# Fixed buffers in place of rotating pools, and a reordered instruction table, in an attention and MLP kernel on one core

## The chip, the core and the metric

The kernel runs on one core of a Trainium2 chip. The metric is the device time of one execution in microseconds (us). The engines named below are PE (TensorE, with PEld for its weight loads), DVE (VectorE), ACT (ScalarE), POOL (GpSimd) and SP (SyncE, which here only issues DMAs).

## The reference

```python
def _attn_ref(q, k, v):
    q_s = np.exp(q - np.max(q, axis=-1, keepdims=True))
    q_s = q_s / (np.sum(q_s, axis=-1, keepdims=True) + 1e-09)
    k_s = np.exp(k - np.max(k, axis=2, keepdims=True))
    k_s = k_s / (np.sum(k_s, axis=2, keepdims=True) + 1e-09)
    kv = np.einsum('bhsd,bhse->bhde', k_s, v)
    return np.einsum('bhsd,bhde->bhse', q_s, kv)      # 8 x 8 heads, 576 rows, 64 columns
def _moe_ref(x, w_in, w_out):                         # x: 4608 x 512, w_in: 512 x 2048
    h = x @ w_in
    sp = np.where(h > 20.0, h, np.log1p(np.exp(np.minimum(h, 20.0))))
    return (h * np.tanh(sp)) @ w_out                  # Mish, then 2048 x 512
```

The output of the attention, with its heads side by side, is x. All inputs are float32.

## The kernel before, in words

**The work.** The attention goes item by item (two heads each, numbers 0 to 31 in the names q16, k16, pkv6 and so on). A query item is loaded (q_load, L346, on SP), its row maxima are reduced on DVE (L392, `qm`), exchanged and subtracted (ACT L379, DVE L383, POOL L224), raised to the exponential (ACT L470, with an ACT table load ahead of it), summed, divided, transposed (DVE L510 and its neighbours) and multiplied on PE (L538, tiles `px` and `pt`). The key side is similar: kt_load (L335, tile `kt_two`, on SP), the exponential on ACT (L458, L473), the product with v on PE (L573, tile `pkv`).

The MLP works on 9 chunks of 512 rows. Each float32 operand is split in a high and a low float32r part, and each product takes three matmuls (high by high, high by low, low by high). Three chunks go through the first product directly (h_part, L629). The other six, in three pairs k = 1 to 3, go through a scheme that computes a 2 by 2 block product with seven block products: first_product (L823) makes the partial products `px`, `py` and `pz` in PSUM, ACT copies them into `g` (L859), DVE adds others (L863), ACT applies Mish (L867). second_product (L839, tiles `qx`, `qy`, `qz`) does the same for w_out, with k = 0 to 3. Its operand `gs` is made from `g`: a mix on DVE where needed (g_mix, L224, `g<-g,g`), a high part on ACT (CAST, L889), a low part on DVE (L224, `gs<-g,gs`). One call of first_product or second_product for one block is six matmuls of 512 columns, which the text calls a product.

**The weights.** The sums of weight blocks that the seven products need (`w_in`, `m_in`, `w_out`, `m_out`: POOL L739, ACT L743, DVE L224) are stored once to a DRAM array `ws` (L704, on SP) and come back by w_fetch (L807, on POOL's own DMA queue) into a ring of six buffers: a fetch waits until PE has read what its buffer held.

**The order.** Nothing here is scheduled automatically. ORDER is a table of 2522 tokens (for example `A1.3.5`: first_product of block 3, product 5, pair 1; `BB0.2.1`: second_product; `LQ16`: the load of q16; `F88`: the fetch of ws88; `GH1.1.1`: the high part of `gs1_1_1`; `DS0.2.1`: a store of output; `LK30`: the load of k30). The program goes through it once, so the table sets the order of the instructions on each engine; across engines they wait on semaphores. BANKS is a second table, of letters, that gives each PSUM tile one of eight banks.

**The pools touched.** Pool `sp` rotates 4 buffers of the tag "wc", first for the unpacked weights (`wc_*`), then for output tiles (`ob*`). Pool `wp` rotates 2 buffers for `m0_*` and `m1_*`. Pool `rp` rotates 4 for `gh*` and 4 for `gl*`. open_sc (token `PS`) closes the pools `rw`, `sp`, `wp` and `rq` and opens the rings s1, s2, s3 and s0, which hold the `gs` tiles of the pairs 1 to 3, in their memory. The first write into that memory, the ACT CAST of `gs1_1_1` (token `GH1.1.1`), waits for the last readers of the closed pools, among them the stores of the `ob0_*` tiles.

Of the kernel before, what the change touches and what calls it, by code (L numbers as in the profile page):

```python
# [33 lines left out]
RB16 RA18 RO14 WK0 RB15 RM20 R31 RB18 RH17 RC16 RM21 QZ5 H29 RA19 RO17 RC15 H30 RH16 RB19 R26 RH15 H31 RC19 QM4 O5  # L34
RC18 Y7 RA23 RO16 RA21 RH18 RB21 RA24 RO18 RC21 O6 RM24 RB23 RB24 RO15 QM5 RC23 H32 RC24 H33 G7 RH24 H34 GL7 RH19 RO24
MK7 H35 MK6 T4 RL26 Y8 O7 RD19 LQ6 TC4 G8 R28 RA20 R27 GL8 RH23 LK8 RB20 RM25 RO23 ST2 RC20 RA22 V6 H40 RH21 RS22 RB22
T5 RO21 H41 RC22 LQ7 TC5 H42 RA25 RH20 RB25 H43 RH22 RO20 RC25 H36 MQ6 R29 RH25 H37 L6 Y10 RD22 H38 RA26 SQ6 G10 WK9
H39 RB26 H44 Y9 RO25 RC26 H45 GL10 H46 RL28 WW8v EQ6 H47 GA9 Q6 XT4 O8 WM8.0p ZT4 RA27 GL9 RM27 ZT5 WM8.1p RA28 RB27
ST5 RM30 RC27 WK8 RH26 O9 MQ7 RB28 SQ7 RC28 WK6 QZ6 EQ7 QM6 H48 WH8.0 Q7 RH28 H49 RO26 WH8.1 H50 RH27 H56 WL8.1 QZ7
RO28 H52 WP8.1 H57 Y11 WL8.0 GA11 H51 QM7 MK8 WP8.0 H58 Y12 WK10 RO27 H53 GA12 GL11 KB8 GL12 H54 WW9v RM29 H59 RA29  # L40
WK12 H55 Y14 RB29 B6 Y13 O10 KS6 GA13 WM9.0p WK1 GL13 WH9.0 WM9.1p RC29 RW30 O11 ST4 GA14 RL31 RB30 RH29 RC30 RW31 KM8
GL14 WL9.0 XP4 RB31 UE8.0 WP9.0 RD29 T6 RH30 RC31 O12 WH9.1 Z5 WL9.1 Z4 WP9.1 TC6 ZL4 EK6 ZL5 WW10v T7 KP6 LQ8 TC7
# [5 lines left out]
LK12 WM12.1p GM20 WH12.0 PK8 WH12.1 WL12.0 WW13v WP12.0 PX8 WL12.1 HM19 EQ10 Z9 LQ11 Q10 Z8 WP12.1 ZL9 MK12 V12 ES0.3
HM31 GM19 ZT9 WM13.0p QW10 QV10 WH13.0 MQ11 QM10 HM16 KB12 ZL8 MS11 T10 WM13.1p WH13.1 MT11 WL13.0 HM26 S10 SQ11
WP13.0 WL13.1 ST9 EQ11 GH0.1.1 LQ12 Q11 WP13.1 HM30 KM12 WW14v UE12.1 WK7 QW11 ZT8 QV11 UE12.0 HM24 QM11 ST8 U12.0 T11  # L50
WM14.0p GM26 MQ12 GM22 U12.1 GM16 HM17 WM14.1p GM24 LK14 ES0.2 WW15v PX10 GM17 WH14.0 PK10 MS12 WL14.0 WP14.0 Z11 HM21
Z10 ZL11 WH14.1 MT12 ZL10 SQ12 ZT10 S12 WL14.1 EQ12 HM40 LQ13 Q12 WP14.1 QW12 WM15.0p GH0.1.0 HM32 GK0.1.1 MK14 GM30
# [1007 lines left out]
```

## Time and profile before

| | before |
|---|---|
| median of 3 runs | 781.46 us (780.98 to 783.69) |
| profiled execution, its own time | 782.3 us |
| its span | 780.5 us |
| granted TensorE clock | 1.000 throughout (2.4 GHz) |
| PE busy | 770.3 us, 99% of the span |
| DVE, ACT, POOL busy | 563.7 us (72%), 511.0 us (65%), 297.3 us (38%) |
| moved by DMA | 192.75 MB, 247 GB/s on average |

Shares are of the span, and an engine counts as busy while one of its instructions runs. PE fills the span almost whole, so the place to look is the few gaps between its instructions.

### The profile page before, as it was taken

To read this page: it belongs to the slowest core of one execution; us is meant where nothing else is said; L and a number is where in the kernel's file an instruction comes from. 1 tells how busy PE (TensorE), PEld (TensorE's weight loads), DVE (VectorE), ACT (ScalarE), POOL (GpSimd) and SP (SyncE) were. 2 spreads that over 40 slices of the span, in tenths; PEclk is the share of its full clock that TensorE was granted. 3 is DMA by queue.
4 is the path that set the end of the run, shared out by engine and by line. 5 is a ranking of instruction groups with operands and counts; after the bars stand their busy time and mean duration, and the time that the engine had idled before them with its cause. 6 is when DMAs were issued, how large, how long until landed. Compare 5 with 4: busy or idle time off the path is not lost.

```text
span 780.5 us, 12662 instructions
## 1 busy us (share of the span) xinstructions
PE 770.3 (99%) x4592; PEld 623.5 (80%) x4592; DVE 563.7 (72%) x877; ACT 511.0 (65%) x952; POOL 297.3 (38%) x378
## 2 busy tenths in 40 slices
PE   8999999999999999999999999999999999999997
...
PEclk9999999999999999999999999999999999999999
...
GB/s 342 399 347 234 299 270 267 229 169 249 267 295 300 293 304 207 311 325 254 218 212 234 239 299 174 236 188 232 191 235 202 252 227 190 163 237 170 240 202 175
DMA packets 80717, 192.75 MB, mean 247 GB/s; under 512 B 16016, under 2 KB 28560, under 8 KB 80656
## 3 DMA queue, kind: packets, MB, share of 16 engines
...
q8 instruction: 36, 0.59, 0.3%
...
## 4 chain that ended last, share of the span: by engine, by line
PE 68%; DVE 9%; ACT 7%; DMA 7%; issue 4%; POOL 3%; SPq 1%; DVEq 0%; POOLq 0%; ACTq 0%
PE px L823 15%; PE qx L839 14%; PE qy L839 8%; PE qz L839 8%; PE py L823 7%; PE ph L629 6%; PE pz L823 4%; DMA ws<-ws 2%; PE po L670 2%; DMA q<-in_qs_dram 2%; DVE gs L224 2%; PE px L538 1%; DMA ws<-m_in 1%; PE pt L573 1%; POOL m_in L739 1%
## 5 line engine op out<-in xcount | busy, mean ns | idle before, releaser
L807 POOL DMA_DIRECT2D ws<-ws x200 | 108.5, 544 | 373.5 <-PE px L823 78.0
L889 ACT CAST gs<-g 128x1024 fp32r<-128x1024 f32 x112 | 116.4, 1052 | 75.4 <-PE qx L839 26.3
L224 DVE TENSOR_TENSOR gs<-g,gs 128x1024 fp32r<-128x1024 f32 x112 | 137.3, 1242 | 37.0 <-ACT gs L889 36.8
L839 PE MATMUL qx<-gs,ws 128*128 128x512 f32 x576 | 136.2, 390 | 0.2 <-DVE gs L224 0.2
L823 PE MATMUL px<-xh,ws 128*128 128x512 f32 x384 | 128.9, 392 | 0.8 <-ACT g L859 0.5
L839 PEld LDWEIGHTS qx<-gs,ws 128*128 128x128 f32 x576 | 107.9, 188 | 23.9 <-issue 0.8
L839 PE MATMUL qz<-gs,ws 128*128 128x512 f32 x384 | 92.2, 391 | 0.7 <-DVE gs L224 0.7
L839 PE MATMUL qy<-gs,ws 128*128 128x512 f32 x384 | 90.9, 390 | 0.3 <-DMA ws<-ws 0.2
L629 PE MATMUL ph<-xs,wi 128*128 128x512 f32 x384 | 90.2, 391 | 0.0
L823 PEld LDWEIGHTS px<-xh,ws 128*128 128x128 f32 x384 | 72.1, 188 | 18.5 <-ACT g L859 1.9
L839 PEld LDWEIGHTS qz<-gs,ws 128*128 128x128 f32 x384 | 71.7, 188 | 16.9 <-DVE gs L224 1.1
L839 PEld LDWEIGHTS qy<-gs,ws 128*128 128x128 f32 x384 | 71.9, 188 | 16.1 <-DMA ws<-ws 0.6
L629 PEld LDWEIGHTS ph<-xs,wi 128*128 128x128 f32 x384 | 71.6, 188 | 16.0 <-issue 1.0
L859 ACT COPY g<-px 128x512 f32<-128x512 f32 x72 | 41.2, 586 | 64.2 <-PE px L823 64.1
L224 DVE TENSOR_TENSOR g<-g,g 128x1024 f32<-128x1024 f32 x64 | 78.3, 1235 | 3.7 <-ACT g L867 2.9
L823 PE MATMUL px<-xl,ws 128*128 128x512 f32 x192 | 74.9, 390 | 0.0
L823 PE MATMUL py<-xh,ws 128*128 128x512 f32 x192 | 65.9, 389 | 0.0
L863 DVE TENSOR_TENSOR g<-py,g 128x512 f32<-128x512 f32 x48 | 32.2, 682 | 41.0 <-PE py L823 20.8
L224 POOL TENSOR_TENSOR q<-q,qm 128x576 f32<-128x576 f32 (+1 forms) x31 | 42.3, 1364 | 29.2 <-DVE qm L383 15.6
L867 ACT ACTIVATE g<-g 128x512 f32<-128x512 f32 x72 | 43.5, 629 | 6.4 <-DVE g L863 6.0
L629 PE MATMUL ph<-xs_odd,wi 128*128 128x512 f32 x192 | 45.1, 391 | 0.0
L629 PEld LDWEIGHTS ph<-xs_odd,wi 128*128 128x128 f32 x192 | 35.8, 188 | 8.3 <-issue 0.8
(169 smaller groups left out, 1267.7 us busy)
## 6 DMA issues: line engine op xcount, KB each, us to landing
ws<-ws POOLq DMA_DIRECT2D x197, 512.0 KB, 4.6
...
ws<-m_out SPq DMA_DIRECT2D x32, 256.0 KB, 2.7
ws<-m_in SPq DMA_DIRECT2D x32, 256.0 KB, 3.8
raw_out<-in_w_dram SPq DMA_DIRECT2D x14, 512.0 KB, 7.7
...
ws<-wi SPq DMA_DIRECT2D x24, 256.0 KB, 5.3
```

The source lines that it names most:

```text
L224: eng.tensor_tensor(out, a, b, ALU.subtract)
L538: nc.tensor.matmul((px, pt)[x][h][o], kvt[a, j], at[e + j]["qT"][x][a], start=True, stop=True)
L573: nc.tensor.matmul(pkv[i][j * D:(j + 1) * D], k, v_two[a, j, c], start=c == 0, stop=c == NR - 1)
L629: nc.tensor.matmul(gs[n], wi[f][:, a, t], x[:, z], start=t == 0 and i == 0, stop=t == HP - 1 and i == 2)
L670: nc.tensor.matmul(po[t], g[a][:, t * P:(t + 1) * P], wo[f][:, z], start=f == 0 and i == 0, stop=f == NF - 1 and i == 2)
L807: nc.gpsimd.dma_start(dst, src)
L823: nc.tensor.matmul(dst, w[:, a, j], xc[k, p][z][:, j].rearrange("p b s -> p (b s)"), start=p in (1, 2, 7) and j == 0 and i == 0, stop=j == ...
L839: nc.tensor.matmul(psb[key, k][m], w[:, a, m], g[z][:, f % 2], start=first and i == 0, stop=f == NH - 1 and i == 2, skip_group_check=p in ...
L859: nc.scalar.copy(g_quad(k, n)[q], psb[1, k, n])
L863: nc.vector.tensor_tensor(g, psb[2 if q == 0 else 7, k, n], g, ALU.add)
L867: nc.scalar.activation(g, psb[1, k, n] if q == 1 else g, AF.Mish)
L889: nc.scalar.copy(t[0], gq[k, h][G_PART[p]])
```

## The change

The rotating pools are replaced by buffers with fixed numbers: a table SLOTS gives each unpacked weight, output tile and `gh`/`gl` tile the one of four buffers that it takes, and the two `wp` buffers are named m0 and m1 instead of turned. The pools hold as many buffers as before. ORDER keeps its first 300 tokens; behind them the same 2222 tokens stand in another order, on average 14 places from where they stood. BANKS has the same letters up to the 69th and others behind. The instructions are the same in number and kind on every engine: PE has 3886 matmuls in both, 3120 of them of 512 columns. 95 of 1282 tiles lie at another address. Lines of the changed file have numbers higher by 5.

```diff
 ORDER = """
...
-WM10.0p OP13.0 V8 S6 WK13 OP13.2 WH10.0 RD30 XT6 U8.0 WM10.1p XP6 ZT6 ZT7 MQ8 OP14.0 ST7 Z6 WL10.0 WH10.1 ST6 OP13.3
...
+OP13.0 LQ8 TC7 WW10v V8 OP14.0 U8.0 XT6 WM10.0p XP6 ZT6 ZT7 ST7 H60 Z7 ST6 WM10.1p Z6 H61 WH10.0 ZL6 H62 UE8.1 ZL7
...
+SLOTS = {"in": "0321330310321010", "out": "0212021323323021", "ob": "3021", "g": "0321032102310231"}
+
+
+def slot(kind, n):
+    return SLOTS[kind][n]
...
-    plain = [tc.tile_pool(name="rw", bufs=1), tc.tile_pool(name="sp", bufs=4)]
+    plain = [tc.tile_pool(name="rw", bufs=1), tc.tile_pool(name="sp", bufs=1)]
...
-        a = sp.tile([P, SM], U32, tag="wc", name=f"wc_{kind}{f}")
+        a = sp.tile([P, SM], U32, tag=f"wc{slot(kind, f)}", name=f"wc_{kind}{f}")
...
-        plain.append(tc.tile_pool(name="wp", bufs=2))
+        plain.append(tc.tile_pool(name="wp", bufs=1))
...
-        plain.append(tc.tile_pool(name="rp", bufs=LAG + 1))
+        plain.append(tc.tile_pool(name="rp", bufs=1))
...
-        hi = pools["rp"].tile([P, SM], F32R, tag="rh", name=f"gh{n}")
+        hi = pools["rp"].tile([P, SM], F32R, tag=f"rh{slot('g', n)}", name=f"gh{n}")
...
-        ob = obs[c, t] = sp.tile([P, DM], F32, tag="wc", name=f"ob{c}_{t}")
+        ob = obs[c, t] = sp.tile([P, DM], F32, tag=f"wc{slot('ob', t)}", name=f"ob{c}_{t}")
...
-        m = mixed[j, s] = pools["wp"].tile([P, 2, 2, 2 * P], F32, tag="st", name=f"m{s}_{kind}{f}")
+        m = mixed[j, s] = pools["wp"].tile([P, 2, 2, 2 * P], F32, tag=f"st{s}", name=f"m{s}_{kind}{f}")
```

What the two tables do to the engines, at three places. In these rows a name ends in the program's own buffer number, which differs between the two kernels, and the changed kernel's line numbers are higher by 5.

**DVE, at the low part of `gs0_2_1_1`**, in the first quarter of the second products of k = 0. `qm16` is the row maximum of q16, `g...` a mix, `m...` a weight sum, `rs14` and `kvt` the end of an item's key side, `qT15` and `odd` transposes. Before:

```order
L492 RECIPROCAL qs15_2776<-qs15_2776 128x18
L509 STREAM_TRANSPOSE qT15_2832<-qe15_2771 128x512
L510 STREAM_TRANSPOSE odd_88<-qe15_2771 128x64
L392 TENSOR_REDUCE qm16_2845<-q16_2778 128x18
L224 TENSOR_TENSOR g0_2_1_2363<-g0_2_3_2560,g0_2_1_2363 128x1024
L224 TENSOR_TENSOR gs0_2_1_1_2848<-g0_1_2_2056,gs0_2_1_0_2847 128x1024
L224 TENSOR_TENSOR m0_in2_2811<-m0_in2_2811 128x2x256
L224 TENSOR_TENSOR gs0_2_2_1_2861<-g0_2_2_1803,gs0_2_2_0_2860 128x1024
```

After:

```order
L229 TENSOR_TENSOR g0_2_1_2371<-g0_2_3_2481,g0_2_1_2371 128x1024
L397 TENSOR_REDUCE qm16_2823<-q16_2724 128x18
L468 STREAM_TRANSPOSE k16_2832<-kt_two_114 128x576
...
L592 RECIPROCAL rs14_2842<-rs14_2842 128x2
...
L514 STREAM_TRANSPOSE qT15_2860<-qe15_2718 128x512
L515 STREAM_TRANSPOSE odd_88<-qe15_2718 128x64
L388 TENSOR_TENSOR qm16_2823<-qm16_2823,sm16_2834 128x18
L229 TENSOR_TENSOR gs0_2_2_1_2858<-g0_2_2_2091,gs0_2_2_0_2857 128x1024
L229 TENSOR_TENSOR gs0_2_1_1_2820<-g0_1_2_2225,gs0_2_1_0_2819 128x1024
```

Before, the low part of `gs0_2_1_1` stands two rows behind the reduce of q16; in the change it stands twelve rows behind. The load of q16 (token `LQ16`) has moved too: between it and the reduce PE has five products before, and a group of 12 more matmuls of h_part on top in the change.

**POOL, at the fetch of ws88**, near the end of the second products of k = 1. `qe27` is a division and `q28` a subtraction of the attention, `ws` rows are fetches. Before:

```order
L496 TENSOR_TENSOR qe27_5145<-qe27_5145,qs27_5163 128x576
L807 DMA ws86_5207<-ws_109 128x1024
L807 DMA ws87_5233<-ws_109 128x1024
L807 DMA ws88_5259<-ws_109 128x1024
L224 TENSOR_TENSOR q28_5154<-q28_5154,qm28_5222 128x576
L807 DMA ws89_5369<-ws_109 128x1024
L807 DMA ws90_5388<-ws_109 128x1024
```

After:

```order
L812 DMA ws86_5208<-ws_109 128x1024
L501 TENSOR_TENSOR qe27_5149<-qe27_5149,qs27_5168 128x576
L812 DMA ws87_5228<-ws_109 128x1024
L812 DMA ws89_5331<-ws_109 128x1024
L229 TENSOR_TENSOR q28_5163<-q28_5163,qm28_5250 128x576
L812 DMA ws88_5351<-ws_109 128x1024
L812 DMA ws93_5384<-ws_109 128x1024
L812 DMA ws91_5394<-ws_109 128x1024
```

The fetches of ws88 and ws89 have changed places, and the subtraction for q28 stands ahead of ws88. On SP, the load of k30 (576 KB) is issued right ahead of the fetch of ws88 in the table before, and two attention steps and four products ahead of it in the change.

**ACT, at the high part of `gs1_1_1`**, in the first products of k = 1. `g1_*` rows are copies out of PSUM and Mish, `sm`, `kw` and `sz` small exchanges of the attention. Before:

```order
L867 ACT_TABLE_LOAD
L867 ACTIVATE g1_1_3_3875<-g1_1_3_3875 128x512
L601 COPY xt20_4310<-pt20_0_4157 128x64
L379 COPY sz22_4312<-qs22_4300 32x18 x4
L867 ACTIVATE g1_2_1_4074<-px1_4_4017 128x512
L859 COPY g1_3_2_4288<-px1_6_4257 128x512
L767 COPY raw2_4265<-px21_4204 128x512
L867 ACTIVATE g1_1_0_3872<-g1_1_0_3872 128x512
L889 CAST gs1_1_1_4346<-g1_1_0_3872 128x1024
L867 ACTIVATE g1_2_0_4073<-g1_2_0_4073 128x512
L867 ACTIVATE g1_2_1_4074<-px1_5_4081 128x512
```

After:

```order
L864 COPY g1_2_0_4021<-px1_5_4034 128x512
L384 COPY kw24_4077<-km24_4042 32x4 x4
L872 ACTIVATE g1_0_3_3739<-g1_0_3_3739 128x512
L864 COPY g1_1_3_3843<-px1_3_3935 128x512
L872 ACTIVATE g1_0_3_3739<-g1_0_3_3739 128x512
L872 ACTIVATE g1_1_0_3840<-g1_1_0_3840 128x512
L894 CAST gs1_1_1_4108<-g1_1_0_3840 128x1024
L872 ACTIVATE g1_1_1_3841<-px1_2_3815 128x512
L864 COPY g1_2_2_4023<-px1_4_4006 128x512
L475 ACT_TABLE_LOAD
L475 ACTIVATE qe21_4124<-q21_3859 128x576
L864 COPY g1_2_3_4024<-px1_4_4006 128x512
```

The CAST of `gs1_1_1` stood behind the work on `px1_6` and now stands right behind that on `px1_4` and `px1_5`, some 20 products earlier in the run of first products; the Mish of `g1_1_1` and two copies out of `px1_4` come right behind it. What it waits for stands on SP, in the change as follows (`m0_in5` and `m1_in5` are weight sums on their way to `ws`, two DMAs each, and `ob0_2_1` is an output tile of the pool `sp`):

```order
L340 DMA kt_two_114<-in_kp_dram 128x1152
L709 DMA ws_109<-m0_in5_3912 128x512 x2
L709 DMA ws_109<-m1_in5_3981 128x512 x2
L927 DMA out_1_dram<-ob0_2_1_3254 128x512
L351 DMA q22_4134<-in_qs_dram 128x576
L361 DMA v3_113<-in_v2_dram 128x1188
```

The store of `ob0_2_1` is issued behind the two stores of `m1_in5`, which wait for that tile's low part on DVE; in the table its token stands right ahead of `PS`, and four products (`A1.4.7`, `A1.3.5`, `A1.2.3`, `A1.4.6`) stand between it and `GH1.1.1`. One more product (`A1.3.3`) stands between `GH1.1.1` and `A1.4.5`, which writes the bank of `px1_4` again and so needs the copy `g1_2_2` out of it, two rows behind the CAST.

## Rows read from the trace of the kernel before

**Rows 1.** The page: the span, the busy time of PE, and PE and its granted clock over the span in 40 slices (tenths).

```profile
span 780.5 us, 12662 instructions
...
PE 770.3 (99%) x4592; PEld 623.5 (80%) x4592; DVE 563.7 (72%) x877; ACT 511.0 (65%) x952; POOL 297.3 (38%) x378
...
PE   8999999999999999999999999999999999999997
...
PEclk9999999999999999999999999999999999999999
```

**Rows 2.** A piece of the chain that ended last, all of it PE: start, us, engine, tile, line, count.

```profile
267.62 9.52 PE qx L839 x42
```

**Rows 3.** What PE waited for, the three largest but those of the first 12 us: total us, times, longest us.

```profile
PE pz L823 <- DMA ws<-ws: 1.2, 1, 1.2
...
PE qz L839 <- DVE gs L224: 0.7, 1, 0.7
PE px L823 <- ACT g L859: 0.5, 2, 0.3
```

**Rows 4.** The timeline of PE at all its waits behind the first 12 us, with a row more around two of them: start us, us, engine, line, operation, tiles, shape, count, and in brackets the idle time ahead of it and what released it.

```profile
106.54 1.28 PE L573 MATMUL pkv<-v,k 64*64 64x66 f32 x72 [0.34 <-ACT k L473]
...
230.52 0.98 PE L839 MATMUL qz<-gs,ws 128*128 128x512 f32 x3 [0.69 <-DVE gs L224]
...
257.99 0.74 PE L839 MATMUL qx<-gs,ws 128*128 128x512 f32 x2 [0.23 <-DVE gs L224]
...
336.96 0.47 PE L823 MATMUL px<-xh,ws 128*128 128x512 f32 x1 [0.28 <-DMA ws<-ws]
...
346.34 0.39 PE L823 MATMUL py<-xh,ws 128*128 128x512 f32 x1
347.01 0.50 PE L823 MATMUL px<-xh,ws 128*128 128x512 f32 x1 [0.28 <-ACT g L859]
347.35 0.39 PE L823 MATMUL px<-xl,ws 128*128 128x512 f32 x1
...
374.49 0.50 PE L823 MATMUL px<-xh,ws 128*128 128x512 f32 x1 [0.27 <-ACT g L859]
...
465.21 0.47 PE L823 MATMUL pz<-xh,ws 128*128 128x512 f32 x1 [1.19 <-DMA ws<-ws]
...
763.14 1.52 PE L839 MATMUL qz<-gs,ws 128*128 128x512 f32 x6
764.75 0.96 PE L839 MATMUL qy<-gs,ws 128*128 128x512 f32 x3
...
772.74 0.73 PE L839 MATMUL qy<-gs,ws 128*128 128x512 f32 x2 [0.22 <-DMA ws<-ws]
```

**Rows 5.** The timelines of SP (the first row, the issue of the load of q16) and of DVE: its wait for that load and what stood behind; then a reduce of q17.

```profile
220.23 1.00 SPq L346 DMA_DIRECT2D q<-in_qs_dram  x1
...
227.44 0.75 DVE L392 TENSOR_REDUCE qm<-q 128x18 f32<-128x576 f32 x1 [2.12 <-DMA q<-in_qs_dram]
228.12 1.22 DVE L224 TENSOR_TENSOR g<-g,g 128x1024 f32<-128x1024 f32 x1
229.25 1.22 DVE L224 TENSOR_TENSOR gs<-g,gs 128x1024 fp32r<-128x1024 f32 x1
...
256.06 0.74 DVE L392 TENSOR_REDUCE qm<-q 128x18 f32<-128x576 f32 x1
```

**Rows 6.** Two fetches: an issue on SP (k30), then the piece of the chain that is the fetch of ws88 behind it (start, us); then the issue of ws43 on POOL.

```profile
456.28 0.33 SPq L335 DMA_DIRECT2D kt_two<-in_kp_dram  x1
...
456.58 8.50 DMA ws<-ws
...
328.94 0.53 POOL L807 DMA_DIRECT2D ws<-ws  x1 [1.12 <-PE px L823]
```

**Rows 7.** DMA issues (kind, count, KB each, median us from issue to landing): of the whole span, and in the last row of the stretch from 333 to 346 us alone.

```profile
ws<-ws POOLq DMA_DIRECT2D x197, 512.0 KB, 4.6
...
out_dram<-ob SPq DMA_DIRECT2D x19, 256.0 KB, 4.7
...
out_dram<-ob SPq DMA_DIRECT2D x3, 256.0 KB, 7.5
```

**Rows 8.** The timeline of ACT: ahead of PE's two waits for a copy out of PSUM (347.01 and 374.49), and ahead of the one for `pkv` (106.54).

```profile
345.85 0.63 ACT L867 ACTIVATE g<-g 128x512 f32<-128x512 f32 x1
346.39 0.57 ACT L859 COPY g<-px 128x512 f32<-128x512 f32 x1
...
373.27 0.69 ACT L470 ACTIVATE qe<-q 128x576 f32<-128x576 f32 x1 [1.21 <-POOL q L224]
373.87 0.57 ACT L859 COPY g<-px 128x512 f32<-128x512 f32 x1
...
105.29 1.20 ACT L473 ACTIVATE k<-k 128x1152 f32<-128x1152 f32 x1
```

**Rows 9.** The timeline of DVE ahead of PE's start at 764.75.

```profile
764.01 0.68 DVE L918 TENSOR_TENSOR g<-qy,g 128x512 f32<-128x512 f32 x1
```

**Rows 10.** The page's groups of instructions: line, engine, operation, tiles, count, busy us, mean ns of one, idle time ahead and what ended most of it.

```profile
L889 ACT CAST gs<-g 128x1024 fp32r<-128x1024 f32 x112 | 116.4, 1052 | 75.4 <-PE qx L839 26.3
...
L859 ACT COPY g<-px 128x512 f32<-128x512 f32 x72 | 41.2, 586 | 64.2 <-PE px L823 64.1
```

More of the change, by code (lines that the diff above doesn't have):

```diff
@@ L33 @@
 RO13 RA17 RA14 RS17 RO12 QZ4 O3 RB14 RB17 Y5 RL23 GA5 RC17 Y6 RC14 RL19 GA6 H28 GL5 R25 O4 RS18 RA16 GL6 RA15 RH14
[L34 to L42, printed above, removed]
@@ L48 @@
[L48 to L52, printed above, removed]
@@ new lines @@
+A1.7.2 F55 C1.6.2 QV22 F58 J1.5.2 QM22 A1.7.6 J1.7.0 N1.5.2 MQ23 A1.7.7 J1.6.0 C1.7.2 MS23 A1.6.5 N1.5.3 MT23 T22
+N1.0.2 GX1.2.0v N1.7.0 BB1.0.1 F59 C1.6.3 SQ23 BB1.1.1 EQ23 A1.7.5 LQ24 Q23 GH1.2.0 F62 F60 J1.6.3 QW23 BB1.2.1
+GK1.2.0 C1.7.3 QV23 A1.6.3 GX1.1.0v A1.6.4 N1.6.1 J1.7.3 QM23 MK26 A1.7.3 F61 MQ24 F63 BB1.3.1 T23 N1.7.1 N1.3.2
+GX1.1.1v BB1.4.1 GH1.2.1 F64 N1.6.0 GK1.2.1 PK22 MS24 GH1.1.3 MT24 J1.6.2 PX22 SQ24 V26 N1.4.3 BB1.5.1 GK1.1.3
+GX1.2.1v A1.7.4 EQ24 ZT22 ST22 BB1.6.1 J1.7.2 LQ25 Q24 N1.7.2 BB1.7.1 GX1.0.1v QW24 F66 F65 N1.7.3 GX1.3.0v BB1.0.2
@@ new lines @@
+GH1.2.2 QV24 XR22 BB1.1.2 S24 N1.6.2 QM24 BB1.2.2 GH1.7.0 GK1.2.2 F67 GH1.2.3 GK1.7.0 BB1.3.2 F68 N1.6.3 GK1.2.3
+BB1.4.2 GH1.7.1 MQ25 BB1.0.7 GK1.7.1 F69 MS25 MT25 BB1.5.2 T24 SQ25 GX1.0.2v EQ25 BB1.6.2 GH1.7.2 LQ26 GX1.3.1v
+BB1.7.2 F70 GK1.7.2 BB1.1.7 GH1.7.3 F71 Q25 GX1.1.2v ZT23 KB26 BB1.2.7 ST23 DP1.0.0 KM26 GH1.6.0 DJ1.0.0 BB1.3.7
+DS1.0.0 UE26.1 GK1.6.0 BB1.4.7 DP1.0.1 GK1.7.3 QW25 BB1.0.6 F73 UE26.0 QV25 MQ26 GH1.6.1 QM25 BB1.5.7 DJ1.0.1 MS26
+DS1.0.1 GX1.2.2v F72 BB1.6.7 GK1.6.1 GH1.6.2 BB1.1.6 F74 XR23 T25 GK1.6.2 BB1.2.6 MT26 U26.0 SQ26 BB1.3.6 U26.1
@@ new lines @@
+F166 A3.5.7 C3.5.3 N3.4.1 N3.4.0 A3.5.3 J3.5.3 F165 J3.3.2 A3.6.2 N3.5.1 A3.6.6 J3.6.0 F167 GX3.1.0v A3.7.1 C3.6.2
+F169 A3.7.2 A3.6.5 A3.6.7 C3.6.3 N3.5.3 C3.7.0 A3.6.3 J3.6.3 F168 N3.5.0 F171 A3.7.7 A3.5.4 A3.7.6 F170 A3.6.4 C3.7.2
+N3.1.2 GH3.1.2 A3.7.5 J3.6.2 F173 F172 GK3.1.2 BB3.0.1 C3.7.3 N3.0.2 J3.7.3 BB3.1.1 J3.7.0 A3.7.3 GH3.2.0 N3.7.0
+GK3.2.0 BB3.2.1 N3.6.1 N3.7.3 GX3.2.0v N3.6.0 BB3.3.1 F175 N3.4.3 F174 N3.7.1 GX3.2.1v BB3.4.1 GH3.1.3 F176 N3.2.2
+GK3.1.3 BB3.5.1 N3.3.2 GH3.2.1 J3.4.2 BB3.6.1 N3.4.2 GK3.2.1 BB3.7.1 J3.5.2 N3.5.2 A3.7.4 N3.6.3 GH3.2.2 BB3.0.2
@@ L160 @@
+abhcefchdcceafhb gbaehdcgefgecfab hgedhbagecagdhfb dcegbechda
 """
```

220 lines of the change are left out of this document (109 added, 111 removed).

## The prediction, made before the changed kernel was run

> **What bounds the kernel now.** The page comes first. PE is busy for 770.3 of 780.5 us, in nearly every slice, and its clock is at the full 2.4 GHz in all of them [rows 1]. A row of the chain that is all PE gives the price of its work: 42 matmuls of 512 columns in 9.52 us, 0.227 us each, so a product of six takes 1.36 us [rows 2]. The change leaves PE the same matmuls, so this part of the time stays. What can move is the time in which PE stands still, and the view of PE's waits shows how little that is and who causes it: fetches of weights, low parts of `gs` from DVE, copies out of PSUM by ACT [rows 3]. The timeline then places each wait [rows 4].
>
> A wait costs more than its bracket. In the rows at 347.01, the matmul ahead starts at 346.34; without a wait the next would start 0.227 us later, at 346.57, and it starts at 347.01, so 0.44 us are lost there, and the next one comes 0.34 instead of 0.227 us later, another 0.11. That makes 0.55 for a bracket of 0.28, so I add 0.27 to every bracket between large matmuls. The nine waits then cost 0.96 (230.52), 0.50 (257.99), 0.55 (336.96), 0.55 (347.01), 0.54 (374.49), 1.46 (465.21) and 0.49 (772.74). Two are not like these: 0.40 for the small matmuls at 106.54 (0.34 and a little restart), and 0.36 at 764.75, which has no bracket but starts 1.61 us behind the start of six matmuls that take 1.36, with 0.11 for the restart. The sum is 5.8 us [rows 4], and this is the most that a new order alone can win: 781.46 - 5.8 = 775.7.
>
> **The change, part by part.** *The buffers with fixed numbers* add no instruction and no byte. By themselves they can move a wait only where a tile comes to another address, 95 of 1282, and where it takes a buffer whose last reader is later. I cost them at nothing beyond what the order shows below; the work that hides a late buffer is the lead of several products that PE has on the unpacking. If that cover were gone, a late `gh` would show as a PE wait for a `ph` or `po` tile, and the trace before has none.
>
> *The low part of `gs0_2_1_1`.* SP issued the load of q16 at 220.23 and the reduce could start at 227.44, 7.2 us later. DVE stood 2.12 us in front of it, and the g-mix and the low part behind it (1.22 each) came too late for PE at 230.52 [rows 4, 5]. In the change a group of 12 matmuls stands in the lead on top, so PE has 9.5 us of work (42 matmuls) between the load's token and the reduce's, where it had 6.8 (30 of them). A load of 7.2 us is then in time. The reduce of q17 (0.74 us, [rows 5]) no longer stands right ahead of the low part needed at 257.99. I take 1.2 of the 1.46 us that these two waits cost, since the change puts ten other small rows ahead of that low part.
>
> *The fetch of ws88.* It took 8.50 us from issue to landing, with 576 KB of k30 issued 0.30 us ahead of it [rows 6]; the median fetch takes 4.6 [rows 7]. In the change that load has a lead of four products and two attention steps on it, some 8 us by PE's work, and the first use of ws88 comes later too. All 1.46 us go. *The fetch of ws43* was issued at 328.94 [rows 6] and needed 8 us later, at 336.96 [rows 4]. By the table PE had six products (8.2 us) between the end of the buffer's last reader and the first use; in the change nine (12.2 us). Its 0.55 go. The fetch behind the wait at 772.74 has the same lead in both, so its 0.49 stay.
>
> *The copies out of PSUM.* The two waits come from ACT doing a Mish (0.63) or an exponential of the attention (0.69, itself late by 1.21 for POOL) just ahead of the copy that PE needs [rows 8]. The cases in which PE has a single product between the product that a copy reads and the next one in its bank go from 22 to 17 in the order. By that count 1.09 x 5/22 = 0.25 us go; if none of the remaining ones meets a busy ACT, all 1.09. I take 0.55. *The wait at 106.54* comes from an exponential of k6 that ACT starts late (1.20 us at 105.29, [rows 8]); it stands earlier in the change: 0.40. *At 764.75* a DVE join (0.68 us at 764.01, [rows 9]) came behind two others; in the change it stands some three products ahead of its use: 0.36.
>
> The gains add up to 1.2 + 1.46 + 0.55 + 0.55 + 0.40 + 0.36 = 4.5 us.
>
> *The new wait: the first write into closed pools.* The CAST of `gs1_1_1` on ACT waits for the store of `ob0_2_1`, and it now stands some 20 products earlier. Let t = 0 be the start of `A1.4.7`. The store is the third issue on SP behind the low part of `m1_in5`; a large issue there takes 0.33 to 1.00 us [rows 5, 6], so I let it leave SP at 1.0. Such a store lands 4.7 us after its issue in the median of 19, 7.5 in a stretch in which others run beside it [rows 7]. That is 5.7 or 8.5. Behind it on ACT come the CAST (1.05), a Mish (0.63) and a copy (0.59) [rows 8, 10], together 2.27, so the copy out of `px1_4` ends at 8.0 or 10.8. PE gets to `A1.4.5`, which needs it, after five products, at 6.8. It stands 1.2 us, or 4.0; and not at all if DVE lets the store go one product earlier. Queued behind that CAST are the exponential of q21, further copies and the next CASTs, and POOL's divisions wait for that exponential. I take 1.5, nearer the median because the new order has fewer loads there (the tokens around it move 4.9 MB where they moved 6.8), and 0.1 for the restart.
>
> By the Trainium skill ("DMA: Bandwidth & Descriptors", section "Anatomy of one DMA — SWDGE (gpsimd) path") a transfer costs about 2.0 us and its bytes at 436 GB/s, an estimate of 2.6 us for the 256 KB of such a store; the section fits another queue than SP's. By it the CAST waits for nothing that PE would notice and this term is 0, for a sum of 777.9. The rows of such stores, at 4.7 and 7.5, stand against it [rows 7], and I go by them.
>
> *New short leads.* A tile in a bank is read by ACT and written anew by PE within 0.5 to 0.9 us of PE's work at three places of the new order (`ph28` to `pt10_1`, `pt6` to `ph15`, `pt4` to `ph13`), where a copy takes 0.59 [rows 10], and once with no product in between (`px2_6`). I price these at 0.3 together, and one wait that I have not found at the mean of the nine, 5.8 / 9 = 0.6. That is 0.9, between 0 and 2.
>
> The sum for the profiled execution: 782.3 - 4.5 + 1.6 + 0.9 = 780.3. That execution was 0.84 us above the median of the runs, so the median is forecast at **779.5 us**, 2.0 us or 0.26% faster. About 0.5% (3.9 us, so 777.55 and 785.4) is what a measurement of this kernel can tell from no change.
>
> **The rivals.** *All gains, no store wait (A).* If the store of `ob0_2_1` leaves a product earlier or lands in 3.5 us, PE sees nothing of it: 781.46 - 4.5 + 0.9 = 777.9, and with no new wait and both copies saved 776.4; the floor is 775.7. For it speaks that DVE, whose low part of `m_in5` lets the stores go, is busy for only 72% of the span [rows 1]; against it speak the rows of 4.7 and 7.5 us [rows 7]. *The store wait is large (B, the other side).* PE's stall is the landing time less 3.5 us. With gains of 4.5 and other costs of 1.0 it decides from a landing of 7.0 us on: the 7.5 us of the crowded stretch give 4.0 of stall and 782.0, and 8.5 us, which a fetch took, give 783.0. For a loss of over 0.5% it would take 10.9 us, longer than any row here. For it speaks that SP has both stores of `m1_in5` right ahead, that the fetch of ws47 on POOL waits for one of these, and that the fetches behind it on POOL's queue are held up too. *The stalls only move (C).* The gains are then given back by other waits a few products later, as each wait lets the other engines catch up: about 781.2. Against it speaks that a new order can remove a lead without taking it elsewhere, since DVE, ACT and POOL are idle a quarter of the span or more [rows 1].
>
> **How the numbers follow.** Main case, gains partly eaten, 777.6 to 781: 0.47. A, to below 777.55: 0.28. B, above 781.5: 0.15, of which 0.07 beyond 785.4 with a store or a cause that I have not seen. C: 0.10. So faster by over 0.5% 0.28, within 0.5% 0.65, slower 0.07. The range from 776.0 (A without its new waits) to 783.0 (B with 8.5 us) leaves out about 2 in 10.
>
> **What would show it.** PE's waits of after should have no line for a fetch over 0.6 us in the first two thirds, none for the low part of `gs` near 230 and 258, and none at 106. A new line `px <- ACT g` with a bracket of about 1 us near 327 would be the store wait: ACT's timeline there would show the CAST of `gs` released by an output DMA. The forecast is wrong if that bracket is over 3.5 or missing, if `pz <- DMA ws` stays, or if waits that I have no place for add up to more than 2 us.

## The result, and the profile after

The changed kernel took 786.59 us in the median of 16 runs (781.12 to 790.57), against 781.49 us for the kernel before in 16 runs (780.74 to 783.69). The ratio is 1.0056, with an interval of 1.0038 to 1.0075: it is slower by about half a per cent, where 779.5 us and a range of 776.0 to 783.0 had been forecast. Its times also lie further apart: 9.5 us between the lowest and the highest, against 3 us before (6.7 us in a later set of 35 runs of the kernel before).

The page of the changed kernel, to be laid beside [rows 1], and the view of PE's waits, beside [rows 3] (total us, times, longest us):

```profile
span 784.8 us, 12692 instructions
...
PE 770.0 (98%) x4592; PEld 623.6 (79%) x4592; DVE 567.1 (72%) x877; ACT 510.3 (65%) x952; POOL 300.3 (38%) x378
```

```profile
PE px L828 <- ACT xh L796: 2.2, 1, 2.2
PE px L828 <- ACT g L864: 2.1, 1, 2.1
PE qz L844 <- DVE gs L229: 1.8, 1, 1.8
PE qz L844 <- DVE ob L923: 1.2, 1, 1.2
...
PE qy L844 <- DMA ws<-ws: 0.9, 1, 0.9
```

PE's work is the same 770 us. The waits at 106, 337, 347, 374, 465 and 765 us [rows 4] are gone, and so are the two for low parts of `gs`, at 230 and 258. Four new ones stand in their place, fewer and larger, and the one for the last fetch, at 772, has grown. The timeline of PE at these five places (start, us, engine, line, operation, tiles, shape, count, idle time and releaser):

```profile
224.83 0.96 PE L844 MATMUL qz<-gs,ws 128*128 128x512 f32 x3 [1.84 <-DVE gs L229]
...
264.97 1.39 PE L844 MATMUL qz<-gs,ws 128*128 128x512 f32 x5 [1.16 <-DVE ob L923]
...
306.30 0.47 PE L828 MATMUL px<-xh,ws 128*128 128x512 f32 x1 [2.21 <-ACT xh L796]
...
350.80 0.50 PE L828 MATMUL px<-xh,ws 128*128 128x512 f32 x1 [2.06 <-ACT g L864]
...
776.72 0.96 PE L844 MATMUL qy<-gs,ws 128*128 128x512 f32 x3 [0.92 <-DMA ws<-ws]
```

With 0.27 us on each bracket, as in the prediction, they cost 2.1, 1.4, 2.5, 2.3 and 1.2 us, 9.5 together, against 5.8 before. That is 3.7 of the 4.3 us between the two spans. The following rows say what stands behind the waits at 224.83 and 350.80. Two are pieces of the chain (start, us): the store of a weight sum, which lands before POOL can mix the next one, and the store of `ob0_2_1`.

```profile
207.30 8.07 DMA ws<-m_in
...
342.13 6.50 DMA out_dram<-ob
```

The others are from the timelines of DVE and ACT. On DVE a low part of a weight sum waits for POOL, and the additions for w_in2 stand ahead of the low part of `gs` that PE then starts with. On ACT the CAST of `gs1_1_1` is released by the store, and a copy out of PSUM two rows behind it ends where PE starts.

```profile
217.00 0.69 DVE L229 TENSOR_TENSOR m_in<-m_in 128x512 fp32r<-128x512 f32 x1 [3.71 <-POOL m_in L744]
...
222.37 1.28 DVE L731 TENSOR_TENSOR w_in<-wi 128x512 f32<-128x512 f32 x2
223.57 1.21 DVE L229 TENSOR_TENSOR gs<-g,gs 128x1024 fp32r<-128x1024 f32 x1
...
348.73 1.04 ACT L894 CAST gs<-g 128x1024 fp32r<-128x1024 f32 x1 [2.40 <-DMA out_dram<-ob]
...
350.17 0.58 ACT L864 COPY g<-px 128x512 f32<-128x512 f32 x1
```

The CAST at 348.73 is the store wait of the prediction, and the last fetch it had counted as unchanged. The other three places it did not name. By the tables, the low part that PE waits for at 224.83 is that of `gs0_2_0_1`: 36 matmuls `qx` ahead of it are six products, and the token behind them is `BB0.0.2`. In the order before, that product stood behind eight.

### The profile page after: what moved, and what is told of

Its sections match the earlier page's. It is cut to its first block, busy times and chain, and to the rows that moved or that the text cites. A ratio compares the mean times of both kernels' runs of the same rounds, so it can differ in the third digit from the quotient of the medians.

```text
span 784.8 us, 12692 instructions
## 1 busy us (share of the span) xinstructions
PE 770.0 (98%) x4592; PEld 623.6 (79%) x4592; DVE 567.1 (72%) x877; ACT 510.3 (65%) x952; POOL 300.3 (38%) x378
## 4 chain that ended last, share of the span: by engine, by line
PE 78%; DVE 10%; DMA 5%; ACT 3%; issue 2%; POOL 2%; SPq 0%; DVEq 0%; POOLq 0%; ACTq 0%
PE px L828 15%; PE qx L844 14%; PE ph L634 10%; PE qz L844 9%; PE qy L844 8%; PE py L828 7%; PE po L675 6%; PE pz L828 4%; DMA ws<-m_in 3%; DVE gs L229 3%; DVE g L229 2%; PE px L543 1%; PE pt L578 1%; DVE w_in L731 1%; DMA ws<-ws 1%
## 5 line engine op out<-in xcount | busy, mean ns | idle before, releaser
L229 DVE TENSOR_TENSOR g<-g,g 128x1024 f32<-128x1024 f32 x64 | 83.0, 1306 | 4.5 <-ACT g L651 2.3
L229 POOL TENSOR_TENSOR q<-q,qm 128x576 f32<-128x576 f32 (+1 forms) x31 | 38.8, 1252 | 28.0 <-DVE qm L388 12.4
L828 PEld LDWEIGHTS py<-xh,ws 128*128 128x128 f32 x192 | 36.0, 188 | 8.3 <-DVE qm L388 0.8
```

Source lines behind the costliest of these rows:

```text
L229: eng.tensor_tensor(out, a, b, ALU.subtract)
L828: nc.tensor.matmul(dst, w[:, a, j], xc[k, p][z][:, j].rearrange("p b s -> p (b s)"), start=p in (1, 2, 7) and j == 0 and i == 0, stop=j == ...
```

## The experiments

Each kernel was timed beside the kernel before on the same chip, which took 781.8 to 782.3 us there. Tokens are moved within ORDER; a diff shows only the token and its new neighbours.

**The changed kernel again.**

> The changed kernel, not edited, for a second profile and for the spread of its times. Theory: its loss sits at five places of the order where PE now stands (near 225, 265, 306, 351 and 777 us; 2.1, 1.3, 2.4, 2.3 and 1.1 us in the first profile), each released by a DMA that lands late, so the second profile shows waits of 0.5 us or more at at least four of the five and a median of 786 to 787. Rival: the five were that one execution's; then the second profile shows its waits elsewhere, for about the same time.

The median was 784.92 us (12 runs, 781.50 to 789.49; ratio 1.0042, 1.0019 to 1.0066). The profiled execution (782.97 us) shows the waits near 224, 264, 347 and 773, but with 0.8, 1.2, 1.6 and 0.7 us in the brackets, and none near 305. Most of the places belong to the order, then, and how long PE stands at each belongs to the execution; only the wait near 264 has the same 1.16 us in its bracket. Over both sets of runs, 28, the mean is 786.0 us.

**The store of `ob0_2_1` earlier.**

```diff
-... WP5.1 SQ21 DS0.2.1 PS A1.4.7 ...
+... DS0.2.0 DS0.0.0 DS0.2.1 A1.1.5 ...
```

> The changed kernel with one token moved: the store of ob0_2_1 (DS0.2.1) is issued behind DS0.0.0, ahead of the weight stores of m_in5. Theory (the CAST of gs1_1_1 waits for this store's landing): the wait of PE near 351 (2.2 us in its bracket) falls under 0.3, and the median falls by 1.5 to 2.3, to about 784.5. Rival (the wait only moves: the CASTs, copies and fetches behind it are late for other reasons): the bracket near 351 goes, but waits of the same sum come up within the next 15 us, and the median stays within 0.8 of 786.6.

The median was 783.80 us (12 runs; ratio 1.0011, 0.9989 to 1.0032; mean 782.9). The wait near 350 is gone, which is the theory; those near 225, 265 and 775 are absent too, though nothing was moved there. The profiled execution is more telling for another place, the fetch of ws28. The piece of the chain that is this fetch (start, us), the timeline of PE behind it, and the same stretch in steps of 2 us (length, busy time of PE, PEld, DVE, ACT and POOL, then the granted clock, the DMA share and GB/s):

```profile
293.74 10.27 DMA ws<-ws
```

```profile
300.28 0.39 PE L828 MATMUL px<-xh,ws 128*128 128x512 f32 x1
304.15 0.77 PE L828 MATMUL px<-xh,ws 128*128 128x512 f32 x1 [3.48 <-DMA ws<-ws]
304.71 0.63 PE L828 MATMUL px<-xl,ws 128*128 128x512 f32 x1
```

```profile
302.00:304.00 2.00, 0.00 (x0) 0.00 (x0) 1.97 (x2) 1.34 (x2) 0.00 (x0) 0.95 0.19 47
304.00:306.00 2.00, 1.85 (x5) 1.50 (x6) 2.00 (x4) 0.00 (x0) 0.00 (x0) 0.50 0.00 0
306.00:308.00 2.00, 2.00 (x8) 1.59 (x7) 2.00 (x3) 0.92 (x3) 0.00 (x0) 0.70 0.00 0
```

Here the fetch took 10.27 us, PE stood for 3.48, and then its clock was granted at half (0.50, the level of 1.2 GHz) until about 307. The six matmuls behind the wait took 2.7 us instead of 1.36. This wait cost its bracket and about 1.5 us on top, half of the 3.1 us that PE worked at this clock.

**The fetch of ws28 earlier.**

```diff
-... PX18 F33 F28 PK18 WW5v ...
+... PX16 F29 F28 KM20 ...
```

> The changed kernel with one token moved: the fetch of ws28 (F28) goes from behind F33 to behind F29, some nine products earlier. Theory (PE at 306.30 stands for the landing of ws28, which took 9.0 us behind two loads of k and v): its wait of 2.2 us falls under 0.4 and the median falls by about 2.2, to 784.4. Rival (PE stands there for the high part of x on ACT, 1.05 us at 305.20, as the view of waits says): the wait stays at 1.5 to 2.2 us, and so does the time, 786.6.

The median was 783.57 us (12 runs; ratio 1.0008, 0.9983 to 1.0033; mean 783.1), and the wait near 306 is gone from the trace. So the releaser that the row at 306.30 names (the cast of `xh`) was the wrong one: PE waited for the fetch (in the trace of the run with the low parts of m_in7 moved, the same wait names the fetch). In the changed kernel's trace POOL issued two fetches in one piece, the second of them ws28:

```profile
296.64 1.05 POOL L812 DMA_DIRECT2D ws<-ws  x2 [1.79 <-PE qy L844]
```

The buffer of ws28 had long been free, 14 products ahead of the first use (`A1.0.1`), but its token stood behind that of ws33, and ws33 waits until PE has read its buffer. The queue held ws28 back until 297.2, four products ahead of that use; in the order before, its token stands twelve ahead. It then landed 9.0 us later, beside loads of k and v.

**The low parts of m_in7 behind the g-mixes.**

```diff
-... QW15 WL7.0 WH7.1 KM16 QV15 WP7.0 GX0.0.1v ... V16 WL7.1 UE16.0 BB0.1.1 GX0.2.0v WP7.1 ...
+... QW15 WH7.1 KM16 QV15 GX0.0.1v ... V16 UE16.0 BB0.1.1 GX0.2.0v WL7.0 WP7.0 WL7.1 WP7.1 ...
```

> The changed kernel with the two low parts of the weight sums m_in7 on DVE (WL7.0, WL7.1, and the stores WP7.0 behind) moved behind the g-mixes GX0.0.1 and GX0.2.0. Theory (DVE stood 3.7 us at 217.0 in front of WL7.0, which waits through POOL for the landing of a weight store, and the g-mixes and low parts behind came late from there to 265): the waits of PE at 224.8 (2.0 in its bracket) and 265.0 (1.2) both fall under 0.4, and the median falls by 2.5 to 3.4, to about 783.6. Rival (DVE has more work there than it can do, and the wait at 217 is only where its slack lies): the wait at 224.8 goes, the one at 265 stays at 1 us or more, and the median falls by 2 at most.

The median was 784.52 us (12 runs; ratio 1.0031, 1.0011 to 1.0052). The wait at 224 had 0.7 us in its bracket, as in the second unedited execution (0.8), and the one near 264 stayed at 1.2: the theory fell, and so did the part of the rival that has the first of them go. DVE no longer stood for the low part, but for a small exchange (`sz`) on ACT, and ACT stood in two casts of the same weight sum:

```profile
214.40 0.62 ACT L748 CAST m_in<-m_in 128x512 fp32r<-128x512 f32 x1 [1.27 <-POOL m_in L744]
215.05 0.86 ACT L384 COPY sz<-qs 32x18 f32<-32x18 f32 x4
217.28 0.62 ACT L748 CAST m_in<-m_in 128x512 fp32r<-128x512 f32 x1 [1.37 <-POOL m_in L744]
```

The late store of the weight sum held POOL, ACT and DVE alike, since each has a token of that sum in its queue. Taking one token out of one queue did not free the others.

**The kernel before again.**

> The kernel before, not edited, for a second profile. Theory (its nine waits are the order's, and each execution has about the same): waits of PE near 230, 258, 337, 347, 374, 465, 765 and 773 us again, the largest near 465 with over 1 us, and a sum of lost time of 5 to 7 us. Rival (waits for DMA landings are that execution's): the waits for weight fetches (337, 465) are absent or under half of what they were, and others of the same kind stand elsewhere.

The median was 781.87 us (12 runs). The waits near 106, 230, 258, 374 and 465 are there again (the last with 1.6 us), those near 337, 347, 765 and 773 are not, and small ones stand near 254 and 330. The sum of the waits is a little smaller; four of the nine places were that execution's. Theory and rival each hold for a part.

**Both single moves.**

> The changed kernel with both single moves: the store of ob0_2_1 ahead of the stores of m_in5, and the fetch of ws28 behind F29. With each move alone the mean fell by about 3 us from 786. Theory (two separate places, each hit in part of the executions, so that their losses add): a median of 780 to 781, no wait near 305 or 350 in the profile, and the waits near 225, 264 and 775 still there. Rival (a stall spares the next one, because the other engines catch up): a median of 782.5 to 783.5, no better than either alone, with longer waits near 225, 264 or 775.

The median was 781.11 us (12 runs, 777.96 to 783.05; ratio 0.9986, 0.9971 to 1.0000). The means are 786.0 unedited, 782.9 and 783.1 with one move each, and 780.9 with both, so two tokens of 2522 are worth 5.1 us, more than the 4 us by which this order had lost. The spread of 5.1 us is no wider than that of the kernel before beside it (6.2 us in 30 runs). The waits that are left are those near 224 (0.2), 264 (1.2) and 770 (0.3).

**DVE relieved.**

```diff
-... WP7.1 UE16.1 WW2v BB0.2.1 GH0.2.0 F6 GK0.2.0 ... LQ17 WM2.1p Q16 ... PK18 ... V18 WW3v ...
+... WP7.1 UE16.1 BB0.2.1 GH0.2.0 F6 GK0.2.0 WW2v ... LQ17 WM2.1p WW3p Q16 ... V18 ...
```

> As the run with both moves, and DVE relieved near 225 to 265: the weight sum w_in3 is added on POOL instead of DVE (two rows of 0.6 us), and w_in2 behind the low part of gs0_2_0_1 instead of ahead of it. Theory (DVE is busy from 217 to 310 without a gap, so that it is late by what it stood idle ahead of that, and PE waits at 225 and 264 for rows that come late by 1 to 2 us): the wait near 225 falls by 1.2, the one near 264 (1.2 in every profile but one) falls under 0.3, and the median is 2 us below that of the run with both moves. Rival (the row at 264 is late for POOL's additions, which slow DVE's rows beside them): the wait near 264 stays or grows and the median is the same.

The median was 781.41 us (12 runs; ratio 0.9997, 0.9984 to 1.0009): no gain. The waits near 225 and 264 are gone, but PE stood 1.0 us near 249 for a fetch, and 0.9 near 771 for the last one. The two additions on POOL took 4.51 us, and the next fetch, of ws13, was held behind them:

```profile
232.24 4.51 POOL L731 TENSOR_TENSOR w_in<-wi 128x512 f32<-128x512 f32 x2
236.69 0.57 POOL L812 DMA_DIRECT2D ws<-ws  x1
```

**The change without its fixed buffers.**

> The code of the kernel before, with its rotating pools, under the changed kernel's tables for order and banks: the change without its fixed buffers. Theory (the buffers cost and win nothing): 785 to 787, as the changed kernel, with the same places of waiting. Rival (a fixed buffer whose last reader is later holds the weight sums or output tiles up): 2 us or more below the changed kernel, without the waits near 225 and 350.

The median was 787.01 us (7 runs; ratio 1.0060, 1.0032 to 1.0088), the same as the changed kernel as far as 7 runs can tell. The rotating pools do neither better nor worse under this order; no run parts the order from the banks. Its profiled execution, of 789.54 us, shows two more stretches of half clock, behind waits of 1.94 us near 304 and 2.01 us near 352 (columns as above):

```profile
303.00:305.00 2.00, 0.91 (x4) 0.81 (x5) 1.97 (x4) 1.68 (x3) 0.00 (x0) 1.00 0.15 32
305.00:307.00 2.00, 2.00 (x7) 1.58 (x6) 2.00 (x3) 0.83 (x3) 0.00 (x0) 0.52 0.00 0
...
353.00:355.00 2.00, 2.00 (x6) 1.60 (x5) 0.75 (x1) 1.56 (x3) 0.00 (x0) 0.50 0.00 0
```

**The kernel before with two tokens moved.**

```diff
-... U28.1 A2.0.1 DJ1.1.0 LK30 F88 DS1.1.0 ... XH2.7 BB1.4.4 XL2.2 ...
+... U28.1 A2.0.1 DJ1.1.0 F88 DS1.1.0 ... XH2.7 BB1.4.4 LK30 XL2.2 ...
-... BB0.6.1 MQ16 GH0.2.1 GX0.2.1v BB0.7.1 GM29 F10 GH0.2.2 GK0.2.1 BB0.0.2 ...
+... BB0.6.1 GH0.2.1 GX0.2.1v BB0.7.1 GM29 F10 GH0.2.2 GK0.2.1 MQ16 BB0.0.2 ...
```

> The kernel before with two tokens moved, to price two gains that the prediction counted: the load of k30 (LK30) goes behind BB1.4.4, so that no load of 576 KB is issued right ahead of the fetch of ws88, and the reduce of q16 on DVE (MQ16) goes behind the low part of gs0_2_1_1 instead of two rows ahead. Theory (each wait has the cause that was named): the wait of PE near 465 (1.2 and 1.6 us in two profiles) falls under 0.4 and the one near 230 (0.7 and 0.3) goes, and the median falls by 1.5 to 2.3, to about 780. Rival for ws88 (its landing is late for other traffic): the wait near 465 stays at 1 us or more. Rival for q16 (DVE has no slack behind 230 and is late anyway): the waits near 254 and 258 grow by what the one near 230 loses.

The median was 779.30 us (12 runs, 777.71 to 781.59), against 781.87 before: 0.9969, with an interval of 0.9957 to 0.9982, the lowest median of all kernels here. Behind the first 12 us PE has two waits left:

```profile
PE pkv L573 <- ACT k L473: 0.3, 1, 0.3
PE px L823 <- ACT g L859: 0.3, 1, 0.3
```

Both causes that the prediction named, the load of k30 beside the fetch of ws88 and the reduce of q16 ahead of the low part, were right: both waits went. These two cost 0.96 and 1.46 in the first profile, 2.4 together, and 2.6 came, with an interval of 1.4 to 3.4; the wait near 258, for which nothing was moved, is absent as well, so that the two numbers are so close is partly luck.

**Relief at another place, and a later last store.** The first two lines of the diff are against the run with DVE relieved.

```diff
-... LQ17 WM2.1p WW3p Q16 ... MK18 QM16 BB0.4.7 ...
+... LQ17 WM2.1p Q16 ... MK18 QM16 WW3p BB0.4.7 ...
-... DJ3.1.1 BB3.2.4 DS3.1.1 BB3.3.4 ... BM3.7.4.0 BM3.4.4.1 ...
+... DJ3.1.1 BB3.2.4 BB3.3.4 ... BM3.7.4.0 DS3.1.1 BM3.4.4.1 ...
```

> As the run with both moves, with w_in2 behind the low part of gs0_2_0_1, w_in3 on POOL but eight products later than in the run before (behind the division for item 16, where POOL stands idle for 3.6 us), and the last store of out_dram from g (DS3.1.1) issued behind the last matmuls, so that it doesn't run beside the fetch of ws199. Theory (the wait near 248 in the run before was ws13, fetched 3.5 us late behind the addition on POOL; the wait near 264 is DVE's backlog): no wait over 0.3 us near 225, 248 and 264, and near 770 under 0.6 instead of 0.4 to 1.5; a median of 779.5 to 780.2, under both kernels. Rival (relief in one place only uncovers the next wait): fetches near 255 to 262 or copies behind 300 take over, and the median stays at 781.

The median was 781.57 us (12 runs; ratio 0.9991, 0.9979 to 1.0004), no better than both moves alone. The fetch near 249 is in time, but the wait near 264 is back at 1.2 us, and that near 773 has grown to 1.6. The timelines of POOL and DVE say why the relief was none:

```profile
248.58 3.52 POOL L731 TENSOR_TENSOR w_in<-wi 128x512 f32<-128x512 f32 x2
...
248.78 2.17 DVE L229 TENSOR_TENSOR g<-g,g 128x1024 f32<-128x1024 f32 x1
250.87 2.32 DVE L229 TENSOR_TENSOR gs<-g,gs 128x1024 fp32r<-128x1024 f32 x1
```

While POOL adds, DVE's rows of 1.22 us [rows 5] take 2.17 and 2.32. What DVE gave to POOL (1.3 us) it paid back in these two rows.

**POOL's additions out of DVE's way.**

```diff
-... BB0.6.6 DJ0.0.0 WM3.0p GH0.5.1 Q17 BB0.7.6 QW17 GK0.5.1 F22 WM3.1p ...
+... BB0.6.6 DJ0.0.0 GH0.5.1 Q17 BB0.7.6 QW17 GK0.5.1 F22 WM3.0p WM3.1p ...
```

> As the run with both moves, and the first weight sum of m_in3 on POOL (WM3.0, two additions) behind the next fetch instead of ahead of it, out of the stretch in which DVE prepares the join that PE waits for near 264. Theory (where POOL adds beside DVE, DVE's rows of 1024 elements take 1.8 to 2.3 us instead of 1.22, and this is the constant 1.2 us of the wait near 264): the two rows of DVE ahead of that join come back to 1.22 us, the wait near 264 goes from 1.2 to under 0.3, and the median falls by about 1.3 from that of the run with both moves (781.1), to about 779.8. Rival (the join is late by DVE's backlog alone): the wait stays over 0.8.

The median was 780.14 us (6 runs; ratio 0.9976, 0.9960 to 0.9993), and the wait near 264 is gone. The median is not clear of that of the run with both moves (0.9986, 0.9971 to 1.0000); the wait is what this run shows. The rows ahead of the join, in the changed kernel's trace on DVE and POOL, and then here on DVE:

```profile
260.52 2.02 DVE L229 TENSOR_TENSOR g<-g,g 128x1024 f32<-128x1024 f32 x1
262.46 1.76 DVE L229 TENSOR_TENSOR gs<-g,gs 128x1024 fp32r<-128x1024 f32 x1
264.14 0.68 DVE L923 TENSOR_TENSOR ob<-qz,ob 128x512 f32<-128x512 f32 x1
...
260.70 0.75 POOL L744 TENSOR_TENSOR m_in<-w_in 128x256 f32<-128x256 f32 x1
261.52 1.62 POOL L744 TENSOR_TENSOR m_in<-m_in,w_in 128x256 f32<-128x256 f32 x1
```

```profile
258.07 1.21 DVE L229 TENSOR_TENSOR g<-g,g 128x1024 f32<-128x1024 f32 x1
259.20 1.21 DVE L229 TENSOR_TENSOR gs<-g,gs 128x1024 fp32r<-128x1024 f32 x1
260.34 0.68 DVE L923 TENSOR_TENSOR ob<-qz,ob 128x512 f32<-128x512 f32 x1
```

The two rows lost 0.8 and 0.55 us to POOL's additions, 1.35 together, and the wait cost 1.4: that is the constant wait near 264. The Trainium skill ("SBUF — State Buffer", section "Who interferes with whom") says that a DVE instruction with two inputs in SBUF contends with a POOL instruction that reads SBUF; these rows agree with it. Which of the two takes longer differs: here DVE's next row of this kind, at 261.60, kept 1.21 us beside an addition of POOL that took 1.65 instead of 0.75. That fits the run with the store moved, which had no wait near 264 either: DVE's two rows took 1.22 us each there, and the addition beside the second took 1.11.

The wait needs a short lead as well. The join ahead of it (`DJ0.0.0`) empties the bank that `BB0.0.3` writes anew; eight products stand between the two tokens in the order before, and one in the change.

**The kernel before with four tokens moved.**

```diff
-... A1.7.6 GX1.1.0v EQ23 A1.7.7 LQ24 C1.7.2 J1.6.3 ...
+... A1.7.6 GX1.1.0v A1.7.7 LQ24 C1.7.2 EQ23 J1.6.3 ...
-... Z5 WL9.1 Z4 WP9.1 TC6 ZL4 EK6 ZL5 ...
+... Z5 WL9.1 EK6 Z4 WP9.1 TC6 ZL4 ZL5 ...
```

> The kernel before with the two moves that paid (LK30 and MQ16 later) and two more of the prediction's gains: the exponential of q23 on ACT behind the copy that PE waits for near 374, and the exponential of k6 ahead of a cast of x, for the wait near 106. Theory (each wait is priced by its bracket and 0.27): both waits go, 0.54 and 0.40, and the median is 0.9 under the run with two moves (779.3), at about 778.4. Rival (what stands behind comes late instead): waits near 376 to 380 or 108 to 112 of the same size, and the same median.

The median was 782.50 us (11 runs; ratio 1.0002, 0.9990 to 1.0014): the two further moves lost all that the first two had won. Both small waits are gone, and two larger ones stand close behind:

```profile
PE pt L538 <- ACT g L867: 1.7, 1, 1.7
...
PE pq L515 <- ACT qTt L530: 1.0, 1, 1.0
```

Behind the wait of 1.7 us, at 386.90, the granted clock is 0.50 from 388 to 391 us, at a cost of about 1.7 us more (half of the 3.4 us at that level). The run does not part the two moves.

The exponential of k6 now stands ahead of the copies of `qT` and `qTt`, which PE needs before `pkv`. The other move can be followed link by link. The exponential of q23 frees the buffer that the load of q24 fills; with its table load it now comes 3.1 us later (373.29, where it was at 370.15 in the run with two moves). SP issues the load at 374.00 instead of 370.87, DVE's reduce stands 1.56 us for it, ACT's exchange stands for the reduce, and a Mish that empties a bank for PE comes late, at 386.27:

```profile
373.29 0.69 ACT L470 ACTIVATE qe<-q 128x576 f32<-128x576 f32 x1
...
374.00 0.33 SPq L346 DMA_DIRECT2D q<-in_qs_dram  x1
...
379.27 0.76 DVE L392 TENSOR_REDUCE qm<-q 128x18 f32<-128x576 f32 x1 [1.56 <-DMA q<-in_qs_dram]
...
380.11 0.85 ACT L379 COPY sm<-qm 32x18 f32<-32x18 f32 x4 [1.90 <-DVE qm L392]
```

Moving the exponential moved the load that waits for the buffer it frees.

## Why the prediction was wrong

**What bounds the kernel** was right: PE's work stayed at 770 us, and the time moved by what PE stood still.

**The step that failed** is the term for waits that had not been found: 0.6 for one such place, 0.9 with the short leads, between 0 and 2. The profile has three such places, near 225, 265 and 306, and they cost 6.0 us (2.1, 1.4 and 2.5). The other terms were off by less: the gains came to 5.3 instead of 4.5, the store wait to 2.3 instead of 1.6, and the last fetch lost 0.7 more. Together PE stood 3.7 us longer, where 2.0 less had been forecast. The prediction's own sign of being wrong, waits without a place of more than 2 us, is what came.

**The gains.** The fetch of ws88, that of ws43, the copies at 347 and 374, the wait at 106 and the one at 765 all went from the profile, 3.9 us by their price, of which the prediction had counted 3.3. But three of the six (337, 347, 765) are not in the second profile of the kernel before either. A gain priced by one execution's wait is an upper bound; the waits that come back in both profiles (106, 230, 258, 374 and 465) were the sure ones, and moving the causes of two of them (230 and 465) alone gave 2.6 us. The gain of ws43 came by luck. Its lead of nine products was counted from when its buffer comes free; its token stands behind that of ws45, whose buffer PE still reads six products ahead of the first use of ws43, and POOL issued the two in one piece at 334.20. By the queue the lead is six products in both orders.

**The waits for DVE.** The gain at the low part of `gs0_2_1_1`, counted as 1.2, came in full: both waits, 1.46 together, are gone, and the load of q16 was in time, as worked out. But the step went no further than that row. In the new order PE needs another low part sooner, that of `gs0_2_0_1`: three products stand between its token and its use instead of five, and the additions for w_in2 (1.28 us) stand right ahead of it on DVE. That is the wait at 224.83. How late it comes differs from execution to execution (1.84, 0.77 and 1.84 us in three profiles, and none in the run without fixed buffers). In the first of them DVE had stood 3.71 us at 217 for a weight store of 8.07 us, but moving that low part left 0.7 us, so that this is the cause is not shown. The join near 264 is the second place: its lead went from eight products to one, and POOL's additions beside DVE's rows took 1.35 us of it. The prediction searched for short leads of banks that ACT empties, and not of those that DVE empties. From 230 to 280 DVE has no gap to catch up in: it is busy for 9.6 to 10.0 of every 10 us there in both kernels. Yet the wait near 264 is not the lateness of 225 handed on, for it is 1.16 us behind a wait of 1.84, of 0.77 and of 0.19 alike.

**The fetch of ws28** is the third place, with 2.5 us. The prediction compared the leads of fetches by when a buffer comes free, and so counted, ws28 has 14 products instead of 15. A lead so counted is no lead when the token stands behind another fetch in POOL's queue. A fetch that is moved past a waiting one has to be counted from that one's issue. With its actual lead of about 6.9 us it met a landing of 8.7 to 10.3 us in four of five executions, and of 6.1 in the one without the wait; the median fetch of 4.7 us says nothing about it.

**The store ahead of `gs1_1_1`** was found and its mechanism was right, though the CAST moved by 13 products in the tables, not some 20, and the wait stands at 350.80, not near 327. The term was sized 1.6; in the five profiles without the edit it was 2.3, 1.9, 2.2 and 2.3, and once none. In the terms of the sum, the copy ended 9.0 us behind the start of `A1.4.7`, between the 8.0 and 10.8 worked out, and PE got there at 7.0 (6.8 worked out). The landing was 6.50 us, between the two bounds of 4.7 and 7.5 [rows 7] and nearer the upper. The reason given for a value near the lower one, fewer bytes around it, did not hold: the four stores of m_in5 and a fetch were still under way, and the mean busy share of the DMA engines from 340 to 350 us was 0.95, where it had been 0.96 before. The estimate of 2.6 us from the Trainium skill ("DMA: Bandwidth & Descriptors", section "Anatomy of one DMA — SWDGE (gpsimd) path") is far from the 6.50 that the trace has. Rival B named the right place but no stall there was long enough to decide alone; it took ws28 as well.

**The last fetch**, ws199, was counted as unchanged and went from 0.49 to 1.2 us, with anything from none to 1.9 in the other profiles of this order. Issuing a store later did not shorten it, and its cause stays open. One rival was not tried: in both orders the fetch of ws196, of 512 KB too, is issued close behind it (in one piece with it at 770.10 in the change), and no product reads ws196.

**The clock** was not in the sum at all. The mean granted clock over the runs is 0.9976 and 0.9982 in the two sets of the changed kernel and 0.9994 in that of the kernel before. By 780 us that is an estimate of 0.9 to 1.4 us, and an upper bound, for the mean also counts what is granted behind PE's last matmul, where a fall costs nothing; in both profiled executions of the changed kernel (0.999) it fell only there. Behind the first 12 us it fell in three of the other profiles, for about 3 us behind a wait: of 3.48 us, of 1.94 and 2.01, and of 1.72.

**The range** failed by its upper end. It let one new wait be large at a time, and there were four, with the last fetch as a fifth. The case that came, a time beyond 785.4 from a cause not seen, had been given 0.07.
